# Attention and two expert layers on one core: softmax sums' 1e-9 on VectorE, a replanned order, and transposes of the last chunk moved

## The chip, the core and the metric

The kernel runs on one core of a Trainium2 chip. The metric is the time of one execution on the device in microseconds, as a median of runs. TensorE (PE) multiplies and transposes, VectorE (DVE), ScalarE (ACT) and GpSimd (POOL) do the rest on SBUF and PSUM, and SyncE (SP) issues most DMAs. Each engine works through its own queue in order and waits on semaphores for the others.

## What is computed

Inputs are q, k, v of 2 batches, 8 heads, 576 positions and 64 columns, in float32. Three stages follow one another:

```python
# attention, per head
scores = q @ k.T / sqrt(64)
scores = where(scores >= scores.max(-1) - tau, scores, -1e9)
attn = exp(scores - scores.max(-1))
attn = attn / (attn.sum(-1) + 1e-9)
x = attn @ v                                   # reshaped to x [1152, 512]
# first layer: 4 experts, 1024 wide, all used, weighted
p = domain_probs / (domain_probs.sum(-1) + 1e-9)
x = sum(p[:, e] * (relu(x @ w1[e]) @ w2[e]) for e in range(4))
# second layer: 2048 wide
h = relu(x @ w_in); out = (h * h) @ w_out
```

## The kernel before

**Precision.** In the two layers each float32 operand is split into a high and a low fp32r part, and a product is three matmuls (high by high, high by low, low by high). The high part is a cast on ScalarE (`whi` L685 of weights, `xhi` L556, `hhi` L760), the low part a subtraction on POOL (`wlo` L688, `xlo` L559) or VectorE (`hlo` L764).

**Attention.** It is cut into twelve jobs (`JOBS`). A job is a pair of heads of one batch (eight pairs, 0 to 7) and one or both groups of query rows, (0,) with 256 rows or (1,) with 320. Batch 0 has one job for each pair and group, batch 1 one for each pair. A job is made of units, 128 query rows of one head (a corner unit holds the last 64 rows of both heads). For a unit PE writes the scores to PSUM (L381 or L395), VectorE takes the negated row maximum `nm` (L400), the threshold `th` comes from it (L405), ScalarE writes the exponential `p` (L414), VectorE masks it in place and sums it (L421, with an accumulator read), 1e-9 is added to the sum `sm` (L443, for two units at once, so two columns, or one for a corner), VectorE takes the reciprocal `r` (L448), POOL multiplies `p` by it (L466, the norm), PE transposes it (L487), ScalarE copies the transposed block to SBUF (`pt`, L492), and when a job's units are there PE multiplies by v (L543) and x is split (L553, L556, L559).

**Two paths.** The fourth entry of a job says which. On the first (`halves`, before: batch 0) the scores are matmuls in float32 with 64 rows of the array for each half (L381), and q is scaled in one instruction. On the second (before: batch 1) q and k are split into high and low parts (L266, L270, L278 on ScalarE, `q_low` L274 and `k_low` L282 on POOL) and the scores use all 128 rows (L395). `ON_POOL` puts the thresholds of the first path on VectorE and those of the second on POOL.

**The layers.** Six experts' halves follow (the second layer's two halves as e = 4 and 5), each half a unit of `unit()`: first matmuls x by weights in column groups of 512, 320 and 320 tokens for four values of f (L753), then chunks of 128 tokens back (L821), accumulated by VectorE (L833). Three of these units start with the first 512 tokens of x alone (`early`), so that their matmuls can fill PE during attention. Between the two layers each chunk of x is transposed again (`turn_x`, L856) and split (L861 on ScalarE, L864 on VectorE); `turn_x` of chunk n comes behind the matmuls of chunk n+1, and that of the last chunk, 8, behind its own.

**What sets the order.** No order is written by hand. Each operation is handed to `op()` with its engine, an assumed time, what it follows, the buffers it takes, a rank and a lag (from its end to the start of a follower on another engine; `own` is the same on its own engine). `plan()` then simulates the engines: it picks the next operation on an engine among those that can start within `SLACK` of the earliest, by the lowest rank, and the instructions are emitted in the order found. Ranks of attention are the job's start value plus ten for each unit plus the entry in `RANKS` (one table for each path); those of weights are `WEIGHTS` minus 10000 plus a running number that starts at 10000. Matmuls of the layers keep their order and rank from 10000 up.

Of the kernel before, what the change touches and what calls it, by code (L numbers as in the profile page):

```python
# [13 lines left out]
ALU = mybir.AluOpType  # L14
# [10 lines left out]
QT = S // P  # L25
# [18 lines left out]

JOBS = [
    (0, (0,), 0.0, True),
    (1, (0,), 0.0, True),
    (2, (0,), 90.0, True),
    (3, (0,), 130.0, True),
    (0, (1,), 250.0, True),  # L50
    (1, (1,), 250.0, True),
    (2, (1,), 270.0, True),
    (3, (1,), 360.0, True),
    (4, (0, 1), 620.0, False),
    (5, (0, 1), 650.0, False),
    (6, (0, 1), 760.0, False),
    (7, (0, 1), 800.0, False),
]

UNITS = [(0, 0, [(0, (256,)), (256, (256,))], True)]  # L60
# [4 lines left out]

RANKS = [
    {
        "q_load": -379, "v_load": -54, "scale": -61, "q_low": -196, "k_high": 160, "k_low": 282, "qk": -672,
        "rowmax": 373, "threshold": 878, "expo": 26, "mask": 367, "addeps": -325, "recip": -103,
        "norm_corner": 70, "norm": -136, "turn": -494, "evac": 54, "turn_rest": -485, "evac_rest": -237,  # L70
        "turn_corner": -323, "evac_corner": -541, "pv": -430, "x_copy": -316, "x_high": 0, "x_low": -653,
    },
    {
        "q_load": -41, "v_load": -111, "scale": -61, "q_low": -326, "k_high": 96, "k_low": -190, "qk": -1215,
        "rowmax": -103, "threshold": -74, "expo": -196, "mask": 107, "addeps": 441, "recip": -634,
        "norm_corner": 338, "norm": -17, "turn": 7, "evac": 376, "turn_rest": -691, "evac_rest": 90,
        "turn_corner": -719, "evac_corner": 105, "pv": -926, "x_copy": -442, "x_high": -536, "x_low": 96,
    },
]
ON_POOL = {"threshold": (False, True), "scale": (False, True)}  # L80
SLACK = 0.05
WEIGHTS = {"load": 10000, "high": 10000, "low": 700}

# [93 lines left out]
def attention_moe_kernel(ctx, tc, qT, kT, kD, vp, tau, probs, wa, wb, wc, wd, out):  # L179
# [56 lines left out]
    def attention(u, gs, r0, halves, lead=False):  # L236
# [47 lines left out]
        if lead:  # L284

            fw = GW[0]

            def piece(n):
                def f():
                    if not n:  # L290
                        tiles["q"] = new(qb, [P, 2, qw], F32, "q")
                        tiles["k"] = new(qb, [P, 3, HW], F32, "k")
                    q, k = tiles["q"], tiles["k"]
                    if n in (0, 2):
                        nc.scalar.dma_start(q[:, n // 2, :fw], qT[u][:, n // 2, q0:q0 + fw])
                    elif n in (1, 3):
                        nc.sync.dma_start(k[:, n // 2:n], kT[u][:, n // 2:n])
                    else:
                        nc.sync.dma_start(q[:, :, fw:], qT[u][:, :, q0 + fw:q0 + qw])
                return f  # L300

            loads = [
                op("SP", t, piece(n), uses=[qb], rank=-3000 + n, lag=3.55)
                for n, t in enumerate((0.45, 0.45, 0.4, 0.9, 1.5)[:5 if qw > fw else 4])
            ]

            def scale_0():
                q = tiles["q"][:, 0, :fw]
                nc.vector.tensor_scalar(q, q, qsc, None, ALU.mult)

            def scale_1():
                q = tiles["q"][:, 1, :fw]
                nc.scalar.activation(q, q, AF.Copy, scale=qsc)

            def scale_rest():
                q = tiles["q"][:, :, fw:]
                nc.scalar.activation(q, q, AF.Copy, scale=qsc)

            parts = [
                op("DVE", 0.3, scale_0, [loads[0], heads["tau"]], [qb], r0 - 50),  # L320
                op("ACT", 0.35, scale_1, [loads[2], heads["tau"]], [qb], r0 - 50),
            ]
            scales = {0: [parts[0], loads[1]], 1: [parts[1], loads[3]]}
            if qw > fw:
                scales[2] = [op("ACT", 0.8, scale_rest, [loads[4], heads["tau"]], [qb], r0 + 10), loads[3]]
        elif halves:
            load = op("SP", 3.0 + (qw > GW[0]) * 1.2, load_q(None), uses=[qb], rank=r0 + rk["q_load"], lag=2.0)
            if ON_POOL["scale"][phase]:
                scales = [op("POOL", 0.1 + 2 * qw / 470, lambda: nc.gpsimd.tensor_mul(
                    tiles["q"], tiles["q"], qsc.unsqueeze(2).to_broadcast([P, 2, qw])),  # L330
                    [load, heads["tau"]], [qb], r0 + rk["scale"])] * 2
            else:
                scales = [op("ACT", 0.02 + 2 * qw / 930, lambda: nc.scalar.activation(
                    tiles["q"], tiles["q"], AF.Copy, scale=qsc),
                    [load, heads["tau"]], [qb], r0 + rk["scale"])] * 2
        else:
            rb_ = Buf("raw")
            load = op("SP", 5.0, load_raw, uses=[rb_], rank=r0 + rk["q_load"], lag=2.0)
            qs = op("ACT", 0.02 + 2 * qw / 1030, q_scaled, [load, heads["tau"]], [rb_], r0 + rk["scale"], own=0.1)
            qh = op("ACT", 0.02 + 2 * qw / 1100, q_high, [qs], [rb_, qb], r0 + rk["scale"], 0.18)  # L340
            ql = op("POOL", 0.02 + 2 * qw / 450, q_low, [qh], [rb_, qb], r0 + rk["q_low"])
            kh = op("ACT", 1.1, k_high, [load], [rb_, qb], r0 + rk["k_high"], 0.2)
            kl = op("POOL", 2.78, k_low, [kh], [rb_, qb], r0 + rk["k_low"])
            scales = [ql, kl]

# [16 lines left out]
        for k in units:  # L362
# [70 lines left out]
            h = op("POOL" if ON_POOL["threshold"][phase] else "DVE", 0.22 if ON_POOL["threshold"][phase] else 0.13, threshold, [m, heads["tau"]], (),  # L433
                   r + rk["threshold"])
            e = op("ACT", 0.635, expo, [m], [sb, pb], r + rk["expo"], 0.16)
            masks[k] = op("DVE", 0.735, mask, [h, e], [sb, pb], r + rk["mask"], 0.17)
            if u < NP and (gs == (0,) or gs == (0, 1)):
                first_masks.append(masks[k])

            if z or corner:  # L440
                def addeps(i=i):
                    sm = sums[i]["sm"]
                    nc.gpsimd.tensor_scalar(sm, sm, 1e-9, None, ALU.add)  # L443

                def recip(i=i):
                    sm = sums[i]
                    sm["r"] = tiny.tile(list(sm["sm"].shape), F32, tag=f"r{i // QT}", name=f"r{u}_{i}")
                    nc.vector.reciprocal(sm["r"], sm["sm"])  # L448

                ms = [masks[x] for x in range(2 * i, k + 1)]  # L450
                ae = op("POOL", 0.16, addeps, ms, (), r + rk["addeps"])
                rc = recips[i] = op("DVE", 0.073, recip, [ae], (), r + rk["recip"], 0.17)

                def norm_corner(pb=pb, i=i):
                    nc.gpsimd.tensor_mul(
                        pb.tile[:, S:], pb.tile[:, QT * P:S], sums[i]["r"].to_broadcast([P, REM]))

                first = [rc]
                if corner:
                    first = [op("POOL", 0.25, norm_corner, [rc], [pb], r + rk["norm_corner"])]  # L460
                for x in range(2 * i, k + 1):
                    y = x % 2

                    def norm(pb=pb, y=y, i=i):
                        p = pb.tile[:, y * S:(y + 1) * S]
                        nc.gpsimd.tensor_mul(p, p, sums[i]["r"][:, y:y + 1].to_broadcast([P, S]))  # L466

                    norms[x] = op("POOL", 1.105, norm, first, [pb], r + y + rk["norm"])
# [7 lines left out]
        for k in units:  # L476
# [18 lines left out]
                    k0 = y * (QT + 1)  # L495
                    nc.scalar.copy(pt(1)[:, k0:k0 + QT, 2 * P:], tb.tile[:, :, y * REM:(y + 1) * REM])

            a = op("PE", 0.45, turn, [norms[k]], [tb, pb, pts[i // 2 if i < QT else 1]], r + rk["turn"], 0.2, "sq")
            evacs[i // 2 if i < QT else 1].append(
                op("ACT", 0.53 if corner else 0.48, evac, [a], [tb, pts[i // 2 if i < QT else 1]], r + rk["evac"], 0.16))  # L500
            if k in (3, 7):
# [30 lines left out]
        for g in gs:  # L532
# [27 lines left out]

            a = op("PE", 0.05 + 10 * w / 288 * 0.242, pv, evacs[g] + [v_load], [ob, pts[g], vb], r + rk["pv"], 0.19, "col")
            c = op("ACT", 0.07 + w / 1066, x_copy, [a], [ob, xb], r + rk["x_copy"], own=0.095)
            hi = op("ACT", 0.07 + w / 1066, x_high, [c], [xb], r + rk["x_high"], 0.22)
            lo = op("POOL", 0.145 + 2.11 * w / 1000, x_low, [hi], [xb], r + rk["x_low"])
            x_done[u, g] = lo
        attention_ops.extend(ops[base:])
# [25 lines left out]
        nc.gpsimd.tensor_mul(pn, pr, psum_e.to_broadcast([P, NCH, E]))  # L592

    heads = {}
    tau_op = op("SP", 0.3, tau_load, rank=-3500, lag=3.8)
    heads["tau"] = op("DVE", 0.3, head, [tau_op], rank=-2000)
    heads["warm"] = op("PE", 4.8, warm, uses=[Buf("tv")], rank=-3000)
    for n, (u, gs, r0, halves) in enumerate(JOBS):
# [105 lines left out]
        return pe_last[0]  # L704

    x2 = {}
    acc_ops = {}
    last_unit = {}

# [19 lines left out]
    def unit_range(e, half, n0, widths, early, gs, gs2, rank):  # L729
        n1 = n0 + sum(widths)  # L730
        firsts = [(n0 + sum(widths[:n]), w) for n, w in enumerate(widths)]
        hb = Buf("ha" if early else "h")
        width = EARLY if early else N
        h_ops = {}
# [6 lines left out]
        for f in range(FH):  # L741
            for t0, step in firsts:
# [3 lines left out]
                for c in range(DC):  # L746
# [7 lines left out]
                                pb.tile, w, m, start=(c == 0 and n == 0), stop=(c == DC - 1 and n == 2))  # L754

                    last = pe(3 * (step / 2400 + 0.0133), mm, x_ready(e, c, t0, t0 + step) + list(gs[f // 2][:2]) + [free_m if early else late], [pb, wsb])
                c0 = t0

                def relu(f=f, c0=c0, step=step, pb=pb):
# [36 lines left out]
        for n in range(n0 // P, n1 // P):  # L796
# [6 lines left out]
            if (e, half) == (E - 1, 1):  # L803
                turned.append(n)
                if len(turned) > 1:
                    turn_x(turned[-2])
        if turned:
            turn_x(turned[-1])

    def chunk(e, half, n, cut, needs, h_ops, hb, gs2):  # L810
        ob = Buf("m")
# [129 lines left out]
```

## Time and profile before

| | us |
|---|---|
| median of 3 runs | 751.67 (751.28 to 752.32) |
| the profiled execution | 752.49 |
| its span, first to last instruction | 750.7 |
| PE busy in it | 737.0 |
| VectorE, ScalarE, POOL busy | 376.6, 311.0, 332.2 |

The span is what the profiler records; some 1.8 us of the execution lie around it. Attention runs until 210 us of the span, the first layer until 549 us, the second until the end. In the rows below, a time at the front is the start within the span, the second number how long an instruction (or several merged ones) took; "x4" is their number, and a bracket behind a row gives the idle time ahead of it and the engine and line that ended it.

### The profile page before, as it was taken

Reading aid. Unit: us, or ns where it says so; the run is one execution under the profiler, and the core shown is the slowest. Engines: PE = TensorE matmul, PEld = TensorE weight load, DVE = VectorE, ACT = ScalarE, POOL = GpSimd, SP = SyncE. Lnnn points to the kernel's source line nnn. Section 1 sums busy time; section 2 is a strip of 40 time slices with the busy share of each in tenths; the row PEclk is TensorE's granted clock in tenths of the full one; section 3 lists DMA queues with packets and bytes.
Section 4 is the critical chain, followed back from the end, with each engine's and each line's share of the span. In section 5 each row is a group of like instructions: output and inputs, shape, how many; then the busy total and the mean of one; then the engine's idle time right before and its main releaser. Section 6 shows DMA issues by size and latency. Waiting matters only on the chain.

```text
span 750.7 us, 10556 instructions
## 1 busy us (share of the span) xinstructions
PE 737.0 (98%) x4118; PEld 621.9 (83%) x4118; DVE 376.6 (50%) x683; ACT 311.0 (41%) x544; POOL 332.2 (44%) x295
## 2 busy tenths in 40 slices
PE   7899999999999999999999999999999999999998
PEld 5556787778788998988989889888888898898887
DVE  6877765567246645645447454545665022222222
ACT  4888786757532332312304223123255351250430
POOL 3798989999542333212204121122056073461530
PEclk9999999999999999999999999999999999999999
DMA  6642334120223543432333424232233020100002
GB/s 219 226 156 93 104 114 152 60 72 18 85 92 106 197 140 102 162 112 102 113 112 100 141 69 142 97 114 78 105 127 114 15 84 29 57 29 28 1 29 98
DMA packets 26001, 74.88 MB, mean 100 GB/s; under 512 B 3040, under 2 KB 5472, under 8 KB 25952
## 3 DMA queue, kind: packets, MB, share of 16 engines
q1 hardware_dynamic: 24368, 71.73, 29.1%
q10 hardware_dynamic: 1584, 2.49, 0.9%
q8 instruction: 32, 0.52, 0.3%
q14 instruction: 17, 0.14, 0.1%
HBM read 63.46 MB, written 10.75 MB: 99 GB/s over the span
## 4 chain that ended last, share of the span: by engine, by line
PE 85%; POOL 9%; DVE 2%; issue 2%; ACT 2%; POOLq 0%; DVEq 0%; ACTq 0%
PE m L821 37%; PE ph L753 36%; POOL p L466 3%; PE tv L543 3%; PE m L753 3%; PE tv L487 2%; PE s L395 2%; POOL wlo L688 2%; PE s L381 1%; DVE nm L400 1%; POOL q L274 1%; POOL k L282 1%; POOL xlo L559 1%; DVE p L421 1%; POOL th L405 1%
## 5 line engine op out<-in xcount | busy, mean ns | idle before, releaser
L688 POOL TENSOR_TENSOR wlo<-wraw,whi 128x1024 fp32r<-128x1024 f32 x60 | 146.7, 2456 | 320.0 <-ACT whi L685 300.3
L753 PE MATMUL ph<-xlo,whi 128*128 128x320 f32 (+1 forms) x528 | 174.9, 331 | 0.0
L753 PE MATMUL ph<-xhi,whi 128*128 128x320 f32 (+1 forms) x528 | 174.9, 331 | 0.0
L753 PE MATMUL ph<-xhi,wlo 128*128 128x320 f32 (+1 forms) x528 | 174.7, 331 | 0.0
L821 PE MATMUL m<-whi,hhi 128*128 128x512 f32 (+1 forms) x388 | 151.0, 389 | 0.0
L821 PE MATMUL m<-wlo,hhi 128*128 128x512 f32 (+1 forms) x388 | 150.3, 387 | 0.0
L821 PE MATMUL m<-whi,hlo 128*128 128x512 f32 (+1 forms) x388 | 150.2, 387 | 0.0
L753 PEld LDWEIGHTS ph<-xhi,whi 128*128 128x128 f32 x528 | 99.1, 188 | 6.4
L753 PEld LDWEIGHTS ph<-xlo,whi 128*128 128x128 f32 x528 | 99.1, 188 | 6.1
L753 PEld LDWEIGHTS ph<-xhi,wlo 128*128 128x128 f32 x528 | 99.1, 188 | 5.9
L685 ACT CAST whi<-wraw 128x1024 fp32r<-128x1024 f32 x60 | 63.1, 1051 | 93.0 <-PE m L821 93.0
L833 DVE SCALAR_TENSOR_TENSOR acc<-m,pn,acc 128x512 f32<-128x512 f32 x63 | 47.3, 750 | 91.4 <-PE m L821 91.4
L821 PEld LDWEIGHTS m<-whi,hlo 128*128 128x128 f32 x388 | 72.9, 188 | 15.1
L821 PEld LDWEIGHTS m<-whi,hhi 128*128 128x128 f32 x388 | 72.9, 188 | 14.4 <-DVE acc L831 0.2
L821 PEld LDWEIGHTS m<-wlo,hhi 128*128 128x128 f32 x388 | 72.9, 188 | 14.2
L760 ACT ACTIVATE hhi<-ph 128x320 fp32r<-128x320 f32 (+1 forms) x84 | 39.8, 475 | 98.1 <-PE ph L753 97.8
L466 POOL TENSOR_TENSOR p<-p,r 128x576 f32<-128x576 f32 x64 | 72.3, 1148 | 6.5 <-DVE r L448 5.3
L764 DVE SCALAR_TENSOR_TENSOR hlo<-ph,hhi 128x320 fp32r<-128x320 f32 (+1 forms) x84 | 44.6, 536 | 59.2 <-ACT hhi L760 59.0
L780 DVE SCALAR_TENSOR_TENSOR u<-ph,u 128x320 f32<-128x320 f32 (+1 forms) x48 | 26.8, 558 | 83.6 <-ACT u L777 83.5
L787 POOL TENSOR_TENSOR hlo<-u,hhi 128x320 fp32r<-128x320 f32 (+1 forms) x48 | 49.6, 1036 | 31.8 <-ACT hhi L783 30.7
L400 DVE TENSOR_REDUCE nm<-s 128x1 f32<-128x576 f32 x67 | 49.1, 752 | 15.1 <-PE s L395 9.6
L421 DVE SCALAR_TENSOR_TENSOR p<-s,th,p 128x576 f32<-128x576 f32 x59 | 47.6, 814 | 15.6 <-POOL th L405 9.2
(90 smaller groups left out, 928.1 us busy)
## 6 DMA issues: line engine op xcount, KB each, us to landing
wraw<-in_wa_dram SPq DMA_DIRECT2D x22, 512.0 KB, 3.5
wraw<-in_wb_dram SPq DMA_DIRECT2D x22, 512.0 KB, 3.7
wide<-in_wc_dram SPq DMA_DIRECT2D x16, 512.0 KB, 4.0
n<-dbl SPq DMA_DIRECT2D x32, 256.0 KB, 3.4
wide<-in_wd_dram SPq DMA_DIRECT2D x16, 512.0 KB, 3.9
wraw<-n SPq DMA_DIRECT2D x16, 512.0 KB, 3.3
v<-in_vp_dram SPq DMA_DIRECT2D x12, 320.0 KB, 3.0
k<-in_kT_dram SPq DMA_DIRECT2D x7, 432.0 KB, 4.5
```

The source lines that it names most:

```text
L400: nc.vector.tensor_reduce(t["nm"], sb.tile[:, :, :HW], AX.XY, ALU.max, negate=True)
L421: nc.vector.scalar_tensor_tensor(p, sb.tile[:, :, :HW], t["th"], p, ALU.is_ge, ALU.mult, accum_out=sm["sm"][:, z:z + 1])
L466: nc.gpsimd.tensor_mul(p, p, sums[i]["r"][:, y:y + 1].to_broadcast([P, S]))
L685: nc.scalar.copy(sb.tile[0], rb.tile)
L688: nc.gpsimd.tensor_sub(sb.tile[1], rb.tile, sb.tile[0].bitcast(F32))
L753: nc.tensor.matmul(pb.tile, w, m, start=(c == 0 and n == 0), stop=(c == DC - 1 and n == 2))
L760: nc.scalar.activation(h_tiles()[0][:, f, c0:c0 + step], pb.tile, AF.Relu)
L764: nc.vector.scalar_tensor_tensor(ol, pb.tile, 0.0, oh.bitcast(F32), ALU.max, ALU.subtract)
L780: nc.vector.scalar_tensor_tensor(ub.tile, pb.tile, 0.0, ub.tile, ALU.max, ALU.mult)
L787: nc.gpsimd.tensor_sub(ol, ub.tile, oh.bitcast(F32))
L821: nc.tensor.matmul(ob.tile, w, m, start=(f == 0 and y == 0), stop=(f == FH - 1 and y == 2))
L833: nc.vector.scalar_tensor_tensor(a, ob.tile, pn[:, n, e:e + 1], a, ALU.mult, ALU.add)
```

## The change

It changes six things. The 1e-9 goes from POOL to VectorE (L443). The thresholds of the second path go from POOL to VectorE (`ON_POOL`). Job 4, the first of batch 1, takes the first path. The start values of ten jobs, both tables of ranks, `SLACK` and the ranks of loads and casts of weights get other values. Some assumed times and lags of the planner change: the load of tau, the masks' and the new add's delay on their own engine, and the delay of POOL behind two casts on ScalarE. Last, `turn_x` of the last chunk is kept in a list and emitted behind the first column group of the next unit's first matmuls.

```diff
 JOBS = [
     (0, (0,), 0.0, True),
-    (1, (0,), 0.0, True),
-    (2, (0,), 90.0, True),
-    (3, (0,), 130.0, True),
-    (0, (1,), 250.0, True),
+    (1, (0,), -50.0, True),
+    (2, (0,), 10.0, True),
+    (3, (0,), 30.0, True),
+    (0, (1,), 200.0, True),
     (1, (1,), 250.0, True),
-    (2, (1,), 270.0, True),
-    (3, (1,), 360.0, True),
-    (4, (0, 1), 620.0, False),
+    (2, (1,), 320.0, True),
+    (3, (1,), 320.0, True),
+    (4, (0, 1), 570.0, True),
     (5, (0, 1), 650.0, False),
-    (6, (0, 1), 760.0, False),
-    (7, (0, 1), 800.0, False),
+    (6, (0, 1), 800.0, False),
+    (7, (0, 1), 840.0, False),
 ]
 RANKS = [
     {
-        "q_load": -379, "v_load": -54, "scale": -61, "q_low": -196, "k_high": 160, "k_low": 282, "qk": -672,
-        "rowmax": 373, "threshold": 878, "expo": 26, "mask": 367, "addeps": -325, "recip": -103,
-        "norm_corner": 70, "norm": -136, "turn": -494, "evac": 54, "turn_rest": -485, "evac_rest": -237,
-        "turn_corner": -323, "evac_corner": -541, "pv": -430, "x_copy": -316, "x_high": 0, "x_low": -653,
+        "q_load": -689, "v_load": 112, "scale": -144, "q_low": -26, "k_high": -270, "k_low": 220, "qk": -634,
+        "rowmax": 111, "threshold": 1025, "expo": 30, "mask": 202, "addeps": -161, "recip": 67,
+        "norm_corner": 139, "norm": -140, "turn": -498, "evac": -73, "turn_rest": -470, "evac_rest": -239,
+        "turn_corner": -378, "evac_corner": -621, "pv": -314, "x_copy": -424, "x_high": 332, "x_low": -549,
     },
...
-ON_POOL = {"threshold": (False, True), "scale": (False, True)}
-SLACK = 0.05
-WEIGHTS = {"load": 10000, "high": 10000, "low": 700}
+ON_POOL = {"threshold": (False, False), "scale": (False, True)}
+SLACK = 0.1
+WEIGHTS = {"load": 1000, "high": 800, "low": 700}
...
-            kh = op("ACT", 1.1, k_high, [load], [rb_, qb], r0 + rk["k_high"], 0.2)
+            kh = op("ACT", 1.1, k_high, [load], [rb_, qb], r0 + rk["k_high"], 0.5)
...
-            masks[k] = op("DVE", 0.735, mask, [h, e], [sb, pb], r + rk["mask"], 0.17)
+            masks[k] = op("DVE", 0.735, mask, [h, e], [sb, pb], r + rk["mask"], 0.17, own=0.22)
...
-                    nc.gpsimd.tensor_scalar(sm, sm, 1e-9, None, ALU.add)
+                    nc.vector.tensor_scalar(sm, sm, 1e-9, None, ALU.add)
...
-                ae = op("POOL", 0.16, addeps, ms, (), r + rk["addeps"])
+                ae = op("DVE", 0.07, addeps, ms, (), r + rk["addeps"], own=0.12)
...
-            a = op("PE", 0.45, turn, [norms[k]], [tb, pb, pts[i // 2 if i < QT else 1]], r + rk["turn"], 0.2, "sq")
+            a = op("PE", 0.46, turn, [norms[k]], [tb, pb, pts[i // 2 if i < QT else 1]], r + rk["turn"], 0.2, "sq")
...
-            hi = op("ACT", 0.07 + w / 1066, x_high, [c], [xb], r + rk["x_high"], 0.22)
+            hi = op("ACT", 0.07 + w / 1066, x_high, [c], [xb], r + rk["x_high"], 0.5)
...
-    tau_op = op("SP", 0.3, tau_load, rank=-3500, lag=3.8)
+    tau_op = op("SP", 0.3, tau_load, rank=-3500, lag=4.25)
...
+    unturned = []
...
+                if unturned:
+                    turn_x(unturned.pop())
                 c0 = t0
...
-        if turned:
-            turn_x(turned[-1])
+        unturned.extend(turned[-1:])
```

The second table of ranks, for the second path, gets new values in the same way.

## Rows read from the trace of the kernel before

**Rows 1.** The page, first part: busy time of PE and other engines.

```profile
PE 737.0 (98%) x4118; PEld 621.9 (83%) x4118; DVE 376.6 (50%) x683; ACT 311.0 (41%) x544; POOL 332.2 (44%) x295
```

**Rows 2.** Stretches: length, busy time (instructions) by engine, granted clock, DMA share, GB/s.

```profile
6.50:54.00 47.50, 39.70 (x283) 25.20 (x279) 40.52 (x109) 38.02 (x64) 34.91 (x40) 0.96 0.60 211
...
100.00:200.00 100.00, 99.58 (x637) 80.31 (x635) 58.09 (x128) 68.37 (x122) 93.76 (x110) 1.00 0.27 87
...
214.00:520.00 306.00, 306.00 (x1620) 272.06 (x1619) 165.16 (x241) 85.15 (x140) 76.39 (x31) 1.00 0.37 121
```

**Rows 3.** Waits of PE, 0 to 30 us: total, times, longest, in us.

```profile
PE tv L487 <- ACT pt L492: 3.5, 2, 2.6
```

**Rows 4.** Waits of PE, 30 to 60 us.

```profile
PE m L753 <- POOL xlo L559: 1.0, 1, 1.0
```

**Rows 5.** Groups by line: count, busy us, mean ns, idle us before and releasers.

```profile
L400 DVE TENSOR_REDUCE nm<-s 128x1 f32<-128x576 f32 x67 | 49.1, 752 | 15.1 <-PE s L395 9.6 <-PE s L381 5.0
L421 DVE SCALAR_TENSOR_TENSOR p<-s,th,p 128x576 f32<-128x576 f32 x59 | 47.6, 814 | 15.6 <-POOL th L405 9.2 <-ACT p L414 5.4
...
L443 POOL TENSOR_SCALAR sm<-sm 128x2 f32<-128x2 f32 (+1 forms) x40 | 8.6, 216 | 20.0 <-DVE p L421 16.5 <-DVE r L448 0.8 <-DVE pm L421 0.5
L448 DVE RECIPROCAL r<-sm 128x2 f32<-128x2 f32 (+1 forms) x40 | 6.2, 159 | 8.8 <-POOL sm L443 8.2
```

**Rows 6.** Thresholds' line: min/median/max ns, first and last start.

```profile
L405 DVE TENSOR_SCALAR th<-nm,tneg x36: 193/208/217, 7.3 to 82.5; 128x1 f32<-128x1 f32 x36
L405 POOL TENSOR_SCALAR th<-nm,tneg x36: 258/268/289, 87.5 to 190.0; 128x1 f32<-128x1 f32 x36
```

**Rows 7.** A VectorE tensor_scalar of 512 columns: its line; one of them; POOL then.

```profile
L637 DVE TENSOR_SCALAR dbl<-wide x32: 416/418/2206, 216.3 to 577.1; 128x512 int32<-128x512 int32 x32
...
216.29 2.21 DVE L637 TENSOR_SCALAR dbl<-wide 128x512 int32<-128x512 int32 x1
...
213.43 4.79 POOL L688 TENSOR_TENSOR wlo<-wraw,whi 128x1024 fp32r<-128x1024 f32 x2 [2.14 <-ACT whi L685]
```

**Rows 8.** Timeline: accumulator reads of two masks, and POOL at those times.

```profile
21.23 0.08 DVE L421 DVE_READ_ACCUMULATOR p<-s,th,p 128x1 f32 x1
...
19.30 2.25 POOL L466 TENSOR_TENSOR p<-p,r 128x576 f32<-128x576 f32 x2 [0.53 <-DVE r L448]
...
46.68 0.08 DVE L421 DVE_READ_ACCUMULATOR p<-s,th,p 128x1 f32 x1
...
45.61 2.26 POOL L466 TENSOR_TENSOR p<-p,r 128x576 f32<-128x576 f32 x2
```

**Rows 9.** Groups by line: low parts of q and k on POOL, second path.

```profile
L274 POOL TENSOR_TENSOR q<-rq,q 64x1280 fp32r<-64x1280 f32 x4 | 11.7, 2929 | 0.3
L282 POOL TENSOR_TENSOR k<-rk,k 128x1216 fp32r<-128x1216 f32 x4 | 11.2, 2802 | 0.2
```

**Rows 10.** Chain of work that ended last: start, us, work (matmuls).

```profile
62.56 1.17 PE s L381 x8
...
68.30 0.65 PE s L381 x8
...
109.76 1.04 PE s L395 x8
...
549.27 25.06 PE ph L753 x144
```

**Rows 11.** Timeline of PE at the last transposes.

```profile
548.62 0.65 PE L856 MATMUL ph<-ident,acc 128*128 128x128 f32 x4 [0.41 <-DVE acc L833]
```

**Rows 12.** Groups by line: split of a transposed chunk of x.

```profile
L864 DVE TENSOR_TENSOR xlo<-ph,xhi 128x512 fp32r<-128x512 f32 x9 | 6.1, 686 | 1.6 <-ACT xhi L861 1.6
...
L861 ACT CAST xhi<-ph 128x512 fp32r<-128x512 f32 x9 | 5.2, 589 | 17.2 <-PE ph L856 17.2
```

**Rows 13.** Two stretches of the start, columns as in rows 2.

```profile
6.00:13.00 7.00, 4.84 (x36) 3.04 (x32) 6.24 (x15) 3.46 (x5) 1.75 (x3) 0.99 0.99 380
13.00:16.20 3.20, 3.20 (x16) 2.21 (x14) 2.72 (x9) 2.00 (x4) 2.16 (x4) 0.50 0.31 121
```

More of the change, by code (lines that the diff above doesn't have):

```diff
@@ L67 @@
     {
-        "q_load": -379, "v_load": -54, "scale": -61, "q_low": -196, "k_high": 160, "k_low": 282, "qk": -672,
-        "rowmax": 373, "threshold": 878, "expo": 26, "mask": 367, "addeps": -325, "recip": -103,
-        "norm_corner": 70, "norm": -136, "turn": -494, "evac": 54, "turn_rest": -485, "evac_rest": -237,
-        "turn_corner": -323, "evac_corner": -541, "pv": -430, "x_copy": -316, "x_high": 0, "x_low": -653,
-    },
-    {
[L74 to L77, printed above, removed]
-    },
-]
-ON_POOL = {"threshold": (False, True), "scale": (False, True)}
-SLACK = 0.05
-WEIGHTS = {"load": 10000, "high": 10000, "low": 700}
+        "q_load": -689, "v_load": 112, "scale": -144, "q_low": -26, "k_high": -270, "k_low": 220, "qk": -634,
+        "rowmax": 111, "threshold": 1025, "expo": 30, "mask": 202, "addeps": -161, "recip": 67,
+        "norm_corner": 139, "norm": -140, "turn": -498, "evac": -73, "turn_rest": -470, "evac_rest": -239,
+        "turn_corner": -378, "evac_corner": -621, "pv": -314, "x_copy": -424, "x_high": 332, "x_low": -549,
+    },
+    {
+        "q_load": -158, "v_load": 105, "scale": -8, "q_low": -534, "k_high": 138, "k_low": -27, "qk": -1187,
+        "rowmax": -381, "threshold": 2, "expo": -246, "mask": 86, "addeps": 163, "recip": -662,
+        "norm_corner": 486, "norm": -12, "turn": 222, "evac": 407, "turn_rest": -780, "evac_rest": 73,
+        "turn_corner": -803, "evac_corner": 100, "pv": -958, "x_copy": -508, "x_high": -558, "x_low": 60,
+    },
+]
+ON_POOL = {"threshold": (False, False), "scale": (False, True)}
+SLACK = 0.1
+WEIGHTS = {"load": 1000, "high": 800, "low": 700}
 class Buf:
```

## The prediction, made before the changed kernel ran

> **What bounds the kernel now.** I read the page's first part before anything else: PE is busy 98% of the span and every other engine half of it or less [rows 1]. An average over the span hides where the missing 13.7 us lie, so the second view is the table of stretches [rows 2]. From 6.5 to 54 us PE is busy 39.7 of 47.5 us, so 7.8 us are idle; from 100 to 200 us 0.4 us of 100; from 214 to 520 us nothing. The reader is to see one thing in it: there is a start in which PE waits, and then a long dense part in which nothing but PE's own work counts. In the dense part POOL is the next busiest, 93.8 of 100 us, and that costs nothing, because the early MoE matmuls fill PE whenever attention is late. What POOL loses there is worth nothing either, unless PE work goes with it.
>
> The third view is who PE waits for in the start. Its longest waits are 3.5 us for ScalarE's copy of a transposed block (two waits, the longer 2.6 us) [rows 3], and later 1.0 us for the low half of x from POOL [rows 4]. Behind those stands VectorE: it is busy 40.5 of the 47.5 us [rows 2], and one unit of scores (128 rows by 576) costs it a row maximum of 0.752, a threshold of 0.208 and a mask of 0.814 us, 1.77 us in all [rows 5, 6]. So the start is paced by VectorE with ScalarE close behind, until x of the first four jobs is ready and matmuls of the MoE can fill PE.
>
> **The 1e-9 on VectorE.** Removed: 40 instructions of 0.216 us on POOL, 8.6 us, before which POOL sat idle 20.0 us, 16.5 us of it for a mask on VectorE. Also removed is the return trip: the reciprocal waited 8.2 us in all for POOL's add [rows 5]. Added: 40 small VectorE instructions. None like them is in the trace; the nearest rows are the reciprocal on the same tile, 0.159 us mean, and VectorE's threshold, 0.193 to 0.217 us [rows 5, 6], so 40 times 0.16 to 0.21 is 6.4 to 8.4 us of VectorE. I take 0.16, because the tile is the reciprocal's. About 11 of the 40 fall into the start: 1.8 us of VectorE there, against its share of the 8.2 us waited for POOL, 11/40 or 2.3 us. Net 0, between -2.3 us (all waits go, the add hides) and +1.8 us (the waits were idle time anyway). The cover is VectorE's 7.0 idle us in the start. Queued behind each add are the next row maximum and mask, and the norms on POOL wait for the reciprocal behind it.
>
> One thing could make these adds far dearer. A VectorE tensor_scalar from SBUF to SBUF on 512 columns takes 0.418 us at the median, but one took 2.206 us: it began at 216.29 us, while POOL was in the second of two subtractions that together ran from 213.43 to 218.22 us, and ended at 218.50, just behind them [rows 7]. So it waited for POOL. The 36 thresholds on VectorE, with one element per row, stayed within 0.193 to 0.217 us though POOL was busy 34.9 of 47.5 us of the start [rows 2, 6]. The added instruction has two elements per row in 32 of its 40 cases and is like neither. The price if it waits for POOL: in the start, six of the ten two-element sums had a POOL instruction running when their last mask ended, with 0.24 to 1.41 us of it still to go, 4.5 us in all. The first of the six is the accumulator read that ends at 21.31 against norms on POOL until 21.55, the last the one that ends at 46.76 against norms until 47.87 [rows 8]. So between 0 and +4.5 us. The forecast takes 0, by the thresholds, which are nearer in size.
>
> The Trainium skill has a rule that speaks against this edit: SBUF — State Buffer, "Who interferes with whom", says that a tensor_scalar in a two-port mode shares ports with GpSimd and that the later of the two waits until the other has finished; Vector Engine (DVE) Microarchitecture Reference, section 5.1, says that two elements per partition from SBUF do run in that mode. The 2.206 us instruction agrees with the first; no run here shows the second. By that rule this term would be the +4.5 us bound and not 0.
>
> **Thresholds of the second phase on VectorE.** Removed: 36 instructions on POOL of 0.268 us, 9.6 us; added: 36 on VectorE of 0.208 us, 7.5 us [rows 6]. POOL's begin at 87.5 us, where PE is dense and VectorE is busy 58.1 of 100 us [rows 2]. Cost 0; the cover is VectorE's free 42%.
>
> **Job 4 by the first path.** Removed from POOL: one q_low of 2.93 and one k_low of 2.80 us [rows 9], and casts on ScalarE. Both lie in the dense part, so worth 0. On PE two units of scores cost 1.17 us by the first path and 1.04 us by the second; the corner costs 0.65 us by the first [rows 10], and by the second, with twice the matmuls of a unit, as much as two units, 1.04 us. Eight units times 0.065 is 0.5 us more, less 0.4 us for the corner: +0.1 us. Where such a unit stands alone between other matmuls it also pays the change of mode, so the upper bound is one more such half, 8 times 0.13 less 0.4, +0.6 us. I take +0.3 us: this is PE work in the dense part, nothing covers it.
>
> **Last chunk's transposes.** In this order PE waits 0.41 us for the accumulation of chunk 8 on VectorE [rows 11], with the first matmuls of the next unit queued behind them. Moved behind the first 512-column group, the wait is covered by that group: four such f steps take 25.06 us, so one takes 6.26 and its 512 of 1152 columns 2.8 us [rows 10]. What is late next is x of chunk 8, wanted by the third group: after the transposes there are 320 of 1152 columns, 1.7 us, to hide a cast of 0.589 and a subtraction of 0.686 us [rows 12], with one relu and one square of the first group queued ahead of them on ScalarE and VectorE. That fits barely. Term -0.4 us, between -0.4 and +0.2 us. ScalarE and VectorE queues see the same instructions; no DMA moves.
>
> **New ranks, job starts, lags.** These reorder in-order queues and change no work. Three of them act where PE waits. ScalarE's copy of transposed blocks goes from 54 (behind the exponential at 26) to -73 (ahead of it at 30): this is the 3.5 us wait of PE. Jobs 1 to 3 come 50 to 100 earlier against job 4 and later, so the first x is complete sooner and the filler starts before 54 us. POOL's x_low is planned 0.5 us behind its cast, not 0.22: this is the 1.0 us wait. Against that, the weights' casts rank 800 instead of 10000 and so go ahead of late copies of jobs 6 and 7; at that time PE has filler. The loads of q, k, v on SP get other ranks, and weights' loads stay behind them. Gain bounds: all of 3.5 + 1.0 = 4.5 us at best; a loss of the same kind if queue heads come to wait elsewhere, for which I take VectorE's 1.8 us above as the size of one. I take two fifths of the 4.5 us, -1.8 us, since a wait removed in a stretch paced by VectorE comes back in part. In that stretch the granted clock also fell to 0.50 of full, the lower level 1.2 GHz, from 13 to 16.2 us, after PE had been busy 4.84 of the 7 us before; PE's 3.2 us of work there would halve without the fall, so up to 1.6 us either way [rows 13].
>
> **Sum.** 0 + 0 + 0.3 - 0.4 - 1.8 = -1.9 us. The profiled execution took 752.49 us, a span of 750.7 and 1.8 around it; it becomes 750.6. That execution is 0.8 us above the median of 751.67, and the median becomes 749.8.
>
> **Rivals.** (1) The order does nothing for PE: a wait removed by ScalarE's new order returns as a wait for VectorE. For it: VectorE has only 7.0 us idle in 47.5. Against it: PE's own waits name ScalarE first. Then the ranks' -1.8 is 0 and the time is 751.6. This is also the case in which the change does not do what it says, since the 1e-9 moves between two engines of which neither is the bound after 54 us. (2) The start gains all of the 4.5 us, because the filler comes early: 0.3 - 0.4 - 4.5 = -4.6, or 747.1, and 745.5 if the clock does not fall either. For it: filler exists only from x of four jobs on. Against it: VectorE's 1.77 us a unit stay. (3) The two-element add waits for POOL and stands in VectorE's queue in front of row maxima: +4.5 us in the start. If half of it falls into VectorE's idle time the time is 749.8 + 2.2 = 752.0; if none does it is 754.3, slower than before. It decides from the point where more than 1.9 us of these waits are not hidden. For it: the one instruction of 2.206 us. Against it: 36 thresholds that did not wait.
>
> **How the numbers follow.** About 0.2%, 1.5 us, is what a measurement of this kernel can tell from no change: faster is below 750.2, slower above 753.2. Chances: the forecast, 748.3 to 751, 0.40, of which 0.05 lie above 750.2; rival 2, 0.13; rival 1, 0.20; rival 3 half hidden, 0.12; rival 3 in full, or another queue head that waits as long, 0.15. Faster 0.35 + 0.13 = 0.48; same 0.05 + 0.20 + 0.12 = 0.37; slower 0.15. The range goes from 746.8, which leaves out the part of rival 2 without the fall of the clock, to 753.6, which leaves out most of rival 3 in full: some 0.18 outside.
>
> **What the changed profile would show.** Right: the PE wait for ScalarE's copy before 30 us under 2 us; PE idle from 6.5 to 54 us under 6.5 us; no PE wait at the last transposes; attention's POOL time down by about 24 us (8.6 + 9.6 + 5.7) with no effect of its own; dense part unchanged. Wrong: adds on VectorE with a maximum near 1 to 2 us beside POOL instructions (rival 3); PE idle in the start unchanged (rival 1); a PE wait for VectorE's low half of x of chunk 8; a longer stretch at half clock.

## The result, and the profile of the changed kernel

The changed kernel takes 757.62 us (median of 6 executions) against 752.0 us for the kernel before beside it: ratio 1.0068, 95% interval 1.0057 to 1.0078. It is 5.6 us slower where 1.9 us faster was forecast, and it lies outside the range. The profiled execution has a span of 755.4 us.

The page's first part and the stretches (length, busy time and instructions of PE, PEld, VectorE, ScalarE, POOL, then granted clock, DMA share, GB/s) answer to [rows 1, 2, 13]:

```profile
PE 739.7 (98%) x4118; PEld 618.7 (82%) x4118; DVE 401.6 (53%) x759; ACT 308.0 (41%) x542; POOL 310.5 (41%) x217
...
6.50:54.00 47.50, 40.39 (x270) 24.09 (x269) 43.73 (x112) 35.14 (x60) 31.85 (x28) 0.93 0.58 203
54.00:100.00 46.00, 42.78 (x297) 27.94 (x297) 40.40 (x97) 34.13 (x69) 32.19 (x29) 1.00 0.32 107
100.00:200.00 100.00, 99.20 (x648) 77.66 (x647) 73.08 (x185) 69.16 (x124) 78.34 (x60) 1.00 0.22 74
...
6.00:12.40 6.40, 4.42 (x30) 2.73 (x28) 5.97 (x15) 3.69 (x6) 0.21 (x1) 1.00 0.99 375
12.40:19.20 6.80, 6.17 (x21) 3.19 (x22) 5.09 (x16) 3.15 (x6) 3.47 (x4) 0.50 0.25 88
```

In the kernel before, the second of these stretches and the one at the lower clock were:

```profile
54.00:100.00 46.00, 45.40 (x321) 31.58 (x322) 32.52 (x84) 37.24 (x72) 39.38 (x46) 1.00 0.26 82
12.90:16.30 3.40, 3.40 (x16) 2.31 (x14) 2.82 (x9) 2.10 (x4) 2.36 (x4) 0.50 0.32 124
```

Two things are to be seen. PE now has 3.2 idle us of 46 between 54 and 100 us, against 0.6 before, where the forecast took the dense part to have begun; and VectorE's busy time rose by 25.0 us (376.6 to 401.6), far above the 13.9 us that 40 adds of 0.16 and 36 thresholds of 0.208 us come to. The add's line says why (minimum, median and maximum in ns; thresholds and reciprocals for comparison, which answer to [rows 5, 6]):

```profile
L443 DVE TENSOR_SCALAR sm<-sm x40: 132/169/2814, 10.4 to 194.2; 128x2 f32<-128x2 f32 x32, 128x1 f32<-128x1 f32 x8
L405 DVE TENSOR_SCALAR th<-nm,tneg x72: 154/209/216, 7.0 to 191.4; 128x1 f32<-128x1 f32 x72
L448 DVE RECIPROCAL r<-sm x40: 148/166/169, 11.9 to 194.4; 128x2 f32<-128x2 f32 x32, 128x1 f32<-128x1 f32 x8
```

An add of two numbers per partition takes up to 2.81 us. The timelines of VectorE and POOL show against what (start, duration):

```profile
87.23 2.92 POOL L274 TENSOR_TENSOR q<-rq,q 64x1280 fp32r<-64x1280 f32 x1 [2.17 <-ACT q L270]
90.52 2.25 POOL L466 TENSOR_TENSOR p<-p,r 128x576 f32<-128x576 f32 x2 [0.37 <-DVE r L448]
...
87.36 2.81 DVE L443 TENSOR_SCALAR sm<-sm 128x2 f32<-128x2 f32 x1
90.20 0.17 DVE L448 RECIPROCAL r<-sm 128x2 f32<-128x2 f32 x1
...
91.80 0.15 DVE L443 TENSOR_SCALAR sm<-sm 128x1 f32<-128x1 f32 x1
```

The two-column add starts 0.13 us into POOL's subtraction and ends at 90.17, with it (90.15). The one-column add at 91.80 lies inside POOL's norms (90.52 to 92.77) and takes 0.15 us. Over the kernel 18 of the 32 two-column adds took over 0.25 us, and what all of them took beyond 0.17 us is 18.0 us: 6.1 before 54 us, 6.5 from 54 to 100, 5.4 later. Each of the 18 ended 0.02 to 0.03 us behind a POOL instruction. None of the eight one-column adds waited. This is rival 3 of the prediction.

PE's waits (total us, times, longest), first 0 to 30 us, then 30 to 60, answer to [rows 3, 4]:

```profile
PE sx L381 <- DVE th L405: 1.7, 1, 1.7
PE tv L487 <- ACT pt L492: 0.9, 1, 0.9
...
PE s L381 <- DVE p L421: 2.7, 5, 0.8
PE tv L487 <- ACT pt L492: 0.3, 1, 0.3
```

The wait for ScalarE's copies went from 3.5 to 0.9 us as forecast, and the wait for POOL's low half of x is gone; in their place PE waits for VectorE. At the last transposes PE has no idle time left (answers to [rows 11]):

```profile
555.93 0.39 PE L755 MATMUL ph<-xhi,wlo 128*128 128x512 f32 x1
556.16 0.60 PE L859 MATMUL ph<-ident,acc 128*128 128x128 f32 x4
556.52 0.39 PE L755 MATMUL ph<-xhi,whi 128*128 128x320 f32 x1
```

### The profile page after: what moved, and what is told of

Same layout as the page of the kernel before. It is cut to its first block, busy times and chain, and to the rows that moved or that the text cites. A ratio compares the mean times of both kernels' runs of the same rounds, so it can differ in the third digit from the quotient of the medians.

```text
span 755.4 us, 10531 instructions
## 1 busy us (share of the span) xinstructions
PE 739.7 (98%) x4118; PEld 618.7 (82%) x4118; DVE 401.6 (53%) x759; ACT 308.0 (41%) x542; POOL 310.5 (41%) x217
## 4 chain that ended last, share of the span: by engine, by line
PE 89%; DVE 8%; ACT 1%; issue 1%; POOL 0%; POOLq 0%; ACTq 0%; DVEq 0%
PE m L824 38%; PE ph L755 35%; PE tv L543 4%; PE m L755 4%; PE tv L487 3%; DVE p L421 2%; PE s L381 2%; DVE sm L443 2%; DVE nm L400 2%; PE s L395 2%; ACT p L414 1%; PE tv L580 1%; PE ph L859 1%; DVE th L405 0%; ACT pt L492 0%
## 5 line engine op out<-in xcount | busy, mean ns | idle before, releaser
L421 DVE SCALAR_TENSOR_TENSOR p<-s,th,p 128x576 f32<-128x576 f32 x59 | 47.3, 813 | 10.5 <-ACT p L414 9.9
```

Source lines behind the costliest of these rows:

```text
L421: nc.vector.scalar_tensor_tensor(p, sb.tile[:, :, :HW], t["th"], p, ALU.is_ge, ALU.mult, accum_out=sm["sm"][:, z:z + 1])
```

## Experiments

Each was timed beside the kernel before on the same chip; its median there was 752.40 us for the first four below; 752.22 for the add back on POOL, the two in the old order and job 4 in the new order; 752.48 for the other four.

**Two one-column adds.** The order of the changed kernel stays; only the form of the add changes.

```diff
-                    nc.vector.tensor_scalar(sm, sm, 1e-9, None, ALU.add)
+                    [nc.vector.tensor_scalar(sm[:, c:c + 1], sm[:, c:c + 1], 1e-9, None, ALU.add) for c in range(sm.shape[1])]
```

> The changed kernel with its planned order untouched; each two-column add of 1e-9 on VectorE is written as two one-column adds. In the changed kernel's trace the eight one-column adds took 0.13 to 0.16 us whatever POOL did, the 32 two-column ones up to 2.81 us, 18 us over 0.17 us in all. Theory A (the adds' waits for POOL cost the time): no add over 0.25 us, and the time falls by 4 to 6 us, to 751.5 to 753.5. Theory B (the new order and the longer stretch at half clock cost it, 12.98 to 19.8 us against 12.9 to 16.3 before): the adds are short as well, but the time stays at 756 to 758.

Measured 750.85 us, 6.8 below the changed kernel; ratio to before 0.9991 (0.9981 to 1.0002). Line and stretches (columns as above):

```profile
L443 DVE TENSOR_SCALAR sm<-sm x72: 133/145/156, 10.9 to 189.3; 128x1 f32<-128x1 f32 x72
...
54.00:100.00 46.00, 46.00 (x323) 29.62 (x321) 37.09 (x112) 34.78 (x70) 33.21 (x31) 1.00 0.35 118
...
13.40:27.00 13.60, 13.35 (x49) 7.95 (x50) 10.27 (x32) 7.88 (x13) 8.27 (x8) 0.50 0.33 118
```

More instructions, none over 0.156 us though 41 of the 72 started with at least 0.3 us of a POOL instruction still to run, and PE's 3.2 idle us are gone. So the adds' waits are the loss, a little more than the whole of it; theory B falls. The longer stretch at the lower clock is not the cause either: in the profiled execution of this form it lasts 13.6 us, twice the changed kernel's 6.8, and that execution still took 752.79 us against 757.67.

**The add left out.** In the changed kernel the 1e-9 is not added (the sums are at least 1, where float32 does not see it).

```diff
-                    nc.vector.tensor_scalar(sm, sm, 1e-9, None, ALU.add)
+                    pass
```

> The changed kernel, same planned order, with the 1e-9 left out (the sums are at least 1, so float32 sums are the same without it). It takes away the adds' waits and their own 32 times 0.16 us. Theory A: within 1 us of the one-column form or a little below, 750.5 to 753. Theory B: 755.5 to 757.5.

Measured 750.47 us, ratio 0.9969 (0.9957 to 0.998): by medians 0.4 us below the one-column form; from 54 to 100 us PE is not idle here either. What cost 6.8 us was the waiting, not the adding.

**Only the add's engine, in the order before.**

```diff
-                    nc.gpsimd.tensor_scalar(sm, sm, 1e-9, None, ALU.add)
+                    nc.vector.tensor_scalar(sm, sm, 1e-9, None, ALU.add)
```

> The kernel before with one edit: the two-column add of 1e-9 is issued on VectorE at the place that the old plan gave it on POOL; all orders else are those of before. Theory A: two-column adds wait for POOL here too (in the trace of before six of ten in the start would find POOL busy, 4.5 us), and the time rises by 2 to 5 us to 754 to 757. Theory B: within 1 us of before.

Measured 755.42 us, ratio 1.0044 (1.0028 to 1.006). The same waits appear without any of the new order:

```profile
L443 DVE TENSOR_SCALAR sm<-sm x40: 143/160/2050, 11.5 to 196.6; 128x2 f32<-128x2 f32 x32, 128x1 f32<-128x1 f32 x8
```

Here eight adds wait, 8.6 us beyond 0.17 us in all (5.3 before 54 us), and the kernel is 3.0 us slower.

**Only the transposes** (the lines around `unturned` in the diff, on the kernel before).

> The kernel before with only the transposes of the last chunk moved behind the first column group of the next unit. In the changed kernel the stretch from the first matmul of the late units to that unit is 0.9 us shorter than before. Both theories: 0.4 to 0.9 us faster than before, 751.1 to 751.6, if that is the transposes' share.

Measured 751.63 us, ratio 0.9993 (0.9982 to 1.0004). The median is 0.8 us lower, which is what was expected, but the interval takes in no change. The traces are sharper: the first matmul of the late units starts here (kernel before first) at

```profile
213.46 0.30 PE L753 MATMUL ph<-xhi,whi 128*128 128x320 f32 x1
...
213.96 0.30 PE L754 MATMUL ph<-xhi,whi 128*128 128x320 f32 x1
```

and from there to the end of the span (750.7 and 750.5 us) it is 537.2 us before and 536.6 with the transposes moved; the changed kernel has 536.6 too (218.88 to 755.4). So the transposes are worth some 0.7 us, and what else differs between the two kernels lies ahead of that matmul.

**The add back on POOL, in the new order.**

```diff
-                    nc.vector.tensor_scalar(sm, sm, 1e-9, None, ALU.add)
+                    nc.gpsimd.tensor_scalar(sm, sm, 1e-9, None, ALU.add)
```

> The changed kernel, same planned order, with the two-column add back on POOL at the place where the plan has it on VectorE. It takes away VectorE's waits for POOL but gives back the trip to POOL and 40 times 0.21 us of its time; POOL's queue now holds adds that were planned elsewhere. Theory A (the waits in VectorE's queue are the loss): 751 to 753, near the one-column form's 750.85, at most 2 us above it. Rival C (the trip between the engines costs as much as the wait): 755 to 758, like the changed kernel.

Measured 763.61 us, ratio 1.0157 (1.0142 to 1.0172): neither expectation held. Waits of POOL and of VectorE, 6 to 214 us:

```profile
POOL sm L443 <- DVE p L421: 24.5, 12, 9.3
...
DVE r L448 <- POOL sm L443: 34.3, 27, 3.7
```

An add stands in POOL's queue where the plan had none, so POOL waits for masks and VectorE's reciprocal waits for POOL: two in-order queues hold each other up. This is not a fair test of POOL against VectorE, because the order was planned for VectorE; the pair in the old order, with the transposes moved, is: 751.63 us on POOL (above), 749.87 on VectorE without the waits (next).

**The old order with a form that does not wait** (transposes moved, two one-column adds on VectorE at the old place), and **the same without the add.**

> The order before, the last transposes moved, and the 1e-9 as two one-column adds on VectorE at the old place. Compared with the one-column form in the new order (750.85) it tells the new order's own worth. Theory D (new ranks, job starts and job 4's path are worth nothing): 750.3 to 751.4, the moved transposes' 0.7 us and at most 0.8 us for the shorter trip. Theory E (the new order gains 1 us or more): 751.7 to 752.6.

> The order before, the last transposes moved, the 1e-9 left out. The partner of the changed kernel without the add (750.47). Theory D: 750 to 750.9. Theory E: 751.3 to 752.2.

Measured 749.87 us, ratio 0.9965 (0.9953 to 0.9977), and 747.72 us, ratio 0.9951 (0.9932 to 0.9969). Both beat both kernels. Both also lie below their theory D: the old order is better than the new one, by 1.0 us with one-column adds (750.85 against 749.87) and by 2.7 us without (750.47 against 747.72). Theory E, a gain of the new order, falls. How much the new order loses is less sure, because part of the 2.7 us is the clock. In the profiled executions without the add it was at the lower level for 3.4 us in the new order (13.9 to 17.3 us) and not at all in the old. At the same mean granted clock of 0.995, four executions in the new order took 750.5 to 751.0 us and one in the old 749.2, which leaves 1.3 to 1.7 us. Moving the add to VectorE in a form that does not wait is worth 1.8 us in the old order (751.63 to 749.87).

One place where the orders differ is the first MoE matmul that can fill PE; the timelines of PE and the stretch of the start without the add, new order first, then the matmul in the kernel before:

```profile
46.26 0.36 PE L755 MATMUL m<-xhi,whi 128*128 128x256 f32 x1
6.50:54.00 47.50, 41.30 (x290) 25.74 (x287) 39.77 (x107) 37.83 (x65) 33.44 (x30) 0.96 0.61 211
...
36.56 0.39 PE L754 MATMUL m<-xhi,whi 128*128 128x256 f32 x1
6.50:54.00 47.50, 40.71 (x302) 25.82 (x302) 41.18 (x114) 39.65 (x68) 35.06 (x31) 1.00 0.60 213
...
38.02 0.39 PE L753 MATMUL m<-xhi,whi 128*128 128x256 f32 x1
```

It comes 9.7 us later in the new order. That this costs time is not shown: PE is idle 6.2 us of the start in the new order and 6.8 in the old, though at the lower clock the same work also fills more time. The second difference is how often PE goes between matmuls that use all 128 rows and columns of the array and those that use 64 (scores of the first path, L381, and the product with v, L543). Counted along PE's timeline before the late units: 82 changes in the new order, 65 in the old.

**What such a change costs.** In the kernel before, 36 short matmuls were put into the dense part ahead of 512-column groups that overwrite them, half of them with 64 rows.

```diff
+                        if c == 0 and not early and t0 == 0:
+                            R = D if f % 2 else P
+                            nc.tensor.matmul(pb.tile[:, :P], hi[:R], xh[:R, :P], start=True, stop=True)
```

> The kernel before with 36 extra matmuls of 128 columns in the dense part, each ahead of a column group of 512 whose result overwrites theirs: 18 with 64 rows of the array, 18 with all 128. PE waits for nothing there, so the start-to-start times price a change between 64 and 128 rows. The new order makes 82 changes of that kind before the dense part, the old one 65. Theory M (a change costs about 0.09 us, from 0.31 against 0.23 us behind a change in the trace of before): the 64-row ones take 0.15 to 0.25 us more than the 128-row ones, there and back, and 17 more changes are some 1.5 us. Theory N (a change costs nothing by itself): less than 0.05 us more. The whole: 2 to 7 us slower than before.

One execution: 762.94 us, 10.5 above the kernel before and so beyond the 2 to 7 expected. The timeline of PE, one of each kind:

```profile
302.83 0.31 PE L756 MATMUL ph<-xhi,wlo 128*128 128x320 f32 x1
303.07 0.33 PE L754 MATMUL ph<-xhi,whi 64*128 64x128 f32 x1
303.33 0.50 PE L756 MATMUL ph<-xhi,whi 128*128 128x512 f32 x1
303.66 0.40 PE L756 MATMUL ph<-xlo,whi 128*128 128x512 f32 x1
...
309.55 0.31 PE L756 MATMUL ph<-xhi,wlo 128*128 128x320 f32 x1
309.69 0.22 PE L754 MATMUL ph<-xhi,whi 128*128 128x128 f32 x1
309.75 0.45 PE L756 MATMUL ph<-xhi,whi 128*128 128x512 f32 x1
310.03 0.39 PE L756 MATMUL ph<-xlo,whi 128*128 128x512 f32 x1
```

From the matmul ahead to the second one behind, start to start, it is 0.83 us with 64 rows (302.83 to 303.66; all 18 alike) and 0.49 with 128 (309.55 to 310.03; the nine behind a group of 320 columns alike): 0.34 us there and back, 0.17 us for a change, above what theory M had. Seventeen more changes at that price would be 2.9 us. That this is near the 2.7 us between the orders without the add proves nothing: part of the 2.7 is the clock, and the same two orders with one-column adds, so with the same 82 and 65 changes, differ by 1.0 us. The price was measured for rows, and for matmuls of 128 columns; most of the counted changes are of rows (66 against 44 borders of L381). How much of the new order's loss these changes are was not shown.

**Job 4.** In the new order with one-column adds job 4 went back to the second path; in the old order without the add it went to the first. Both were planned anew.

```diff
-    (4, (0, 1), 570.0, True),
+    (4, (0, 1), 570.0, False),
```

> The changed kernel with one-column adds and job 4 on the second path again, so planned anew with the new ranks. The prediction gave the first path +0.3 us (0.1 to 0.6) on PE and nothing on POOL. If that holds: within 0.6 us of the one-column form's 750.85. If POOL's 5.7 us of low parts or ScalarE's casts reach PE after all: 1 to 3 us slower, 752 to 754.

```diff
-    (4, (0, 1), 620.0, False),
+    (4, (0, 1), 620.0, True),
```

> The order before, transposes moved, 1e-9 left out, and job 4 on the first path, planned anew with the old ranks. The prediction: +0.3 us (0.1 to 0.6), so 747.8 to 748.4. In the new order the first path was 2.4 us better than the second (750.85 against 753.25); if that holds for the path itself and not for the order: 744.8 to 746. If the path's changes between 64 and 128 rows count: 748.5 to 750.

Measured 753.25 us (ratio 1.0019, 1.0008 to 1.0029), 2.4 us worse than the first path in the new order; and 751.22 us (0.9987, 0.9974 to 1.0), 3.5 us worse than the second path in the old one, where none of the three expectations held. So the path has no price of its own that carries from one order to another: in both cases the set of ranks did better with the path that it came with. In the old order the changes went from 65 to 78, 2.2 us at 0.17. In the new order they went from 82 to 72, and the time rose all the same; so the count of changes does not decide it, and the cause is open.

**Thresholds of the second path on VectorE** (old order, without the add).

```diff
-                engine = nc.gpsimd if ON_POOL["threshold"][phase] else nc.vector
+                engine = nc.vector
```

> The order before, transposes moved, 1e-9 left out, and the thresholds of the second path on VectorE at their old places. The prediction put this term at 0, since PE is dense from 87 us on and VectorE has room. If so: within 0.8 us of the same kernel without it, 747 to 748.5. If POOL's 9.6 us reach PE after all: 745 to 747; if VectorE's 7.5 us do: 748.5 to 751.

Measured 747.79 us against 747.72 without: nothing, as predicted. The 72 one-column thresholds took 0.217 us at most, so none waited, and POOL's 9.6 us are off the path.

**The add with two inputs from SBUF.** As the one-column form in the old order, but one tensor_tensor of two columns.

```diff
+    eps_t = const.tile([P, 2], F32, name="eps_t")
+    nc.vector.memset(eps_t, 1e-9)
...
+                    nc.vector.tensor_add(sm, sm, eps_t[:, :sm.shape[1]])
```

> As the one-column form in the old order (749.87), but the 1e-9 added by one VectorE tensor_tensor of two columns with a constant tile, so with two inputs from SBUF. Theory A in the narrow form (only the two-column tensor_scalar waits for POOL): no add over 0.25 us and 749.3 to 750.3. In the wide form (two SBUF inputs wait as well): adds of up to 1 to 2.4 us, and 752 to 754.5.

Measured 754.44 us, ratio 1.0038 (1.0019 to 1.0057); its line:

```profile
L445 DVE TENSOR_TENSOR sm<-sm,eps_t x40: 142/154/2075, 11.5 to 196.8; 128x2 f32<-128x2 f32 x32, 128x1 f32<-128x1 f32 x8
```

The wide form holds: two inputs from SBUF wait for POOL as well, and cost as much as the two-column tensor_scalar in the same place (755.42, there without the moved transposes). With two inputs even a one-column add waited, until POOL's norms ended at 67.25 us:

```profile
66.80 0.47 DVE L445 TENSOR_TENSOR sm<-sm,eps_t 128x1 f32<-128x1 f32 x1
...
65.00 2.25 POOL L468 TENSOR_TENSOR p<-p,r 128x576 f32<-128x576 f32 x2 [1.88 <-DVE r L450]
```

## Why the prediction was wrong, step by step

**The sum as measured.** By the medians above: transposes -0.8 (752.40 to 751.63), the add on VectorE without waits -1.8 (to 749.87), the new order with job 4 +1.0 (to 750.85), the waits of the two-column adds +6.8 (to 757.62). The steps come from two series, whose kernels before differ by 0.2 us, so a step is good to some tenths; how long the clock stayed low adds to that for the new order.

**The 1e-9, the step that failed.** The text named the mechanism, priced it at 0 to +4.5 us and took 0, by the thresholds as the nearest row. That neighbour was chosen by size. What decides is the form: a tensor_scalar of one element per partition never waited (72 thresholds, 72 one-column adds), one of two elements did, a tensor_tensor of two inputs did with two elements and with one, and a reciprocal of two did not. The one row that showed a wait, 2.206 us [rows 7], was the same operation with more than one column, so it was the nearer one. The Trainium skill (SBUF — State Buffer, "Who interferes with whom", and Vector Engine (DVE) Microarchitecture Reference, section 5.1) put two-element tensor_scalars among those that wait; the trace agrees, with 2.81 us beside the 0.17 us median.

The bound was too low as well. The waits before 54 us were 6.1 us and not 4.5, and the text counted none later because PE seemed dense from there. Another 6.5 us of waiting from 54 to 100 us took that cover away: PE's idle time there is 3.2 us with the waits and 0 without. The dense stretch was dense only in the old timing; PE's waits of the changed kernel from 60 to 214 us, 3.2 us in all, are all for VectorE's masks.

**The add's own cost and the trip to POOL.** 0.16 us for an add was right (0.157 to 0.170 without a wait). The net of 0 between -2.3 and +1.8 became -1.8 by medians in the old order, inside its bounds.

**The thresholds** at 0 and **POOL's lost work** at 0 were right: POOL is busy 21.7 us less (some 24 were forecast), and the thresholds by themselves changed nothing (747.79 against 747.72).

**The transposes** were put at -0.4 (to +0.2); the median says -0.8, the traces -0.7, more than the bound of -0.4. The feared wait for x of chunk 8 is not there: the third group starts without one.

**Job 4** at +0.3 was mis-sized: a change between 64 and 128 rows there and back costs 0.34 us where the text had 0.13 for a unit that stands alone, and with replanning the term is -2.4 or +3.5 us, by the order it stands in.

**The new order** at -1.8 had the wrong sign: +1.0 to +2.7 by medians, some of it the clock. The named wait did go (3.5 to 0.9 us), but in the changed kernel VectorE's took its place, which was rival 1's mechanism; PE's idle time from 6.5 to 54 us went only from 7.8 to 7.1 us, where under 6.5 was to be the sign. The reading of the job starts failed: earlier starts for jobs 1 to 3 were to bring the filler before 54 us, but in the kernel before it already starts at 38.0 us, and without the add its first matmul came at 46.3 us in the new order and 36.6 in the old. Changes of the array's mode, which the text priced for job 4 alone, rose by 17, and by only seven with job 4 on the second path. Which of these makes the loss stays open: ranks, job starts (nine were changed, not ten), `SLACK` and lags were not taken apart.

**The clock** fell as before, now for 6.8 us instead of 3.4 in the profiled execution, to the lower level, after PE had been busy 4.42 of the 6.4 us ahead of it.

## What to carry to other kernels

Before a small operation moves from one of two engines to the other, look in the trace for an instruction of the same form running beside the engine it leaves, not for one of the same size: here two columns instead of one made 0.17 us into up to 2.8. An in-order engine pays such a wait with everything queued behind it, and a stretch in which TensorE looks dense in the old trace need not be dense behind such waits. When a reorder is priced, count also how often it makes TensorE change between partial and full use of the array, though here that count alone did not give the time.

## What the runs showed of the hardware that was not expected

- A VectorE instruction on two numbers per partition, tensor_scalar or tensor_tensor from SBUF to SBUF, can stand until POOL's instruction ends: 2.81 and 2.08 us at most, against 0.16 to 0.17 us. Written as two one-column tensor_scalars of 0.145 us each it never did, nor did the reciprocal of two columns (at most 0.169 us). A one-column tensor_tensor with two inputs did, 0.47 us.
- A 64-row matmul between 128-row ones costs 0.34 us more than a 128-row one of the same width in its place (0.83 against 0.49 us over three matmuls).
- How long the clock stays at the lower level in the start varies between executions of one kernel, here by some 1.6 us of the time: with one-column adds in the new order, six executions with a mean granted clock of 0.995 to 0.997 took 750.7 to 751.0 us, four with 0.991 took 752.1 to 752.8.
